# GpSimd squares and low halves in pieces of 128 columns, and a bank of the globals read by one VectorE instruction

## The chip, the core and the metric

The kernel runs on one core of one Trainium2 chip. The metric is device time in microseconds (us) of one execution, all transfers included. The engines are named as the profile names them: PE is TensorE's matmul, PEld its weight load, DVE is VectorE, ACT is ScalarE, POOL is GpSimd, SP is SyncE.

## The reference

Windowed attention with a few global tokens feeds a two-layer network whose middle is h·cos(h). Batch 8, 8 heads of 64, 512 local and 32 global positions; then 8 x 544 = 4352 tokens go through 512 -> 2048 -> 512. All inputs are float32.

```
k_all = concat([k_g, k_l]); v_all = concat([v_g, v_l])
out_g = softmax(q_g @ k_all.T / 8) @ v_all                    # 32 global rows see everything
s_ll  = where(|i - j| <= 32, q_l @ k_l.T / 8, -1e9)           # a local row sees a window
out_l = softmax(concat([q_l @ k_g.T / 8, s_ll])) @ v_all
x = concat([out_g, out_l], axis=2)      # as (tokens, 512)
h = x @ w_in                            # 512 -> 2048
return (h * cos(h)) @ w_out             # 2048 -> 512
```

## The kernel before

**Precision.** Operands are split into a float16 high and low half, and each product is made of three matmuls: high·high, high·low, low·high. So a tile that goes into a product is written twice: its high half by ScalarE, its low half by VectorE or GpSimd as value minus high half.

**Two streams that share the engines.** The attention stream works on one batch b at a time, in four pairs of heads p: scores `ps`, a masked row minimum on VectorE (the `CUSTOM_DVE_ANT_0` rows, t and mn), exponentials on ScalarE (`t<-t,mn`), the scaled probabilities in two halves (`planes`), a DMA transpose, the product with v (`acc`), which is written out as `xh` and `xl`. The globals of two pairs (g = 0 or 1) go together: scores `gps`, probabilities `gt` and `planes_g`, a DMA transpose `ptg`, and the product with v in one PSUM bank, `gacc`. The network stream takes what attention has finished in chunks c of 256 tokens (two to a batch, c = 0 to 15; c = 16 is the globals of all batches) and in 8 tiles j of 2 x 128 hidden columns. One tile (c, j), 128 x 512 values, goes through

- `m1_a`: 24 matmuls of 256 columns into a PSUM bank `ph` (three banks, so that (c, j) takes the bank of the tile three before it),
- `m1_b`, `m1_c`: `u` on ScalarE, `u` again on VectorE, the sine `w` on ScalarE (the phase of the cosine at half the angle),
- `m1_d`: the square of w on GpSimd, `gf` = (w - 0.5)·ph on VectorE, which is the last reader of the bank ph, then the high half `gh` on ScalarE and the low half `gl` = gf - gh on GpSimd,
- `m2_a`: 12 matmuls of 512 columns from gh and gl into the two banks `po`, three slots later; of each three, the third needs gl.

In the text below "square" is the GpSimd row `w<-w`, and a tile is written as its row with two numbers: gf(8, 3).

**Splitting on GpSimd.** `pool_tt(o, a, b, op, n)` issues one GpSimd instruction for each n columns. For chunks 0 and 1 n is 128 (`PSQ`, `PSG`); for c of 2 and more n is the whole width, 512.

**The bank of the globals.** `g_f` writes 40 matmuls into `gacc` as [128, pair a, half n, 32]: half 0 takes the products with the high half of the probabilities and the ones with v's low half, half 1 those with their low half. `g_g` empties it with two VectorE instructions, both of which read the bank: x = half 1 · pv, then x = half 0 · pv + x. gacc shares three banks, tag "att", with the scores: ps, gps and acc take the bank that was freed three allocations earlier.

**What sets the order.** The program is written out in slots (`at(slot, phase, f, ...)`). Their rank is a priority, and a scheduler orders the instructions of each engine by it and by its own estimate of when each can start. So an edit that changes an instruction's length can move others. Within an engine instructions then run strictly in that order.

Of the kernel before, what the change touches and what calls it, by code (L numbers as in the profile page):

```python
# [10 lines left out]
F32 = mybir.dt.float32  # L11
# [3 lines left out]
AF = mybir.ActivationFunctionType  # L15
ALU = mybir.AluOpType
AX = mybir.AxisListType
PSUM = bass.MemoryType.PSUM

P = 128  # L20
B = 8
H = 8
SL = 512
SG = 32
D = 64
NPAIR = H // 2
# [50 lines left out]
PSQ = 128  # L77
PSG = 128
# [18 lines left out]
QB = 2  # L97
QH = "A"
FB = 3
s_sc0 = -6  # L100
s_sc2 = -5
s_ex = -4
# [41 lines left out]
def body(tc, qf, v, wi, wo, mask, out):  # L144
    nc = tc.nc
    from contextlib import ExitStack

    with ExitStack() as ctx:
        cp = ctx.enter_context(tc.tile_pool(name="cp", bufs=1))
# [14 lines left out]
        for i in range(4):  # L164
            t = cp.tile([P, 2, 2, 256], F16, name=f"planes{i}")
# [13 lines left out]
        xgs = cp.tile([P, NPAIR], F32, name="xgs")  # L179
        gam = cp.tile([P, 1], F32, name="gam")  # L180
        hsc = cp.tile([P, 1], F32, name="hsc")
        osc = cp.tile([P, 1], F32, name="osc")
        xg = cp.tile([P, NPAIR, B * SG], F32, name="xg")
        pvs = cp.tile([P, B], F32, name="pvs")

        def behind(ins, what, why="scale_first"):
# [41 lines left out]
        def pool_tt(o, a, b, op, n=SPLIT):  # L228

            w = o.shape[-1]  # L230
            k = -(-w // n)
            while w % k:
                k += 1
            for i in range(k):
                c = slice(i * (w // k), (i + 1) * (w // k))
                nc.gpsimd.tensor_tensor(o[..., c], a[..., c], b[..., c], op=op)  # L236
# [302 lines left out]
        def sc_a(b, p, i):  # L539
# [3 lines left out]
            nb, np_ = (b, p + 1) if p < 3 else (b + 1, 0)  # L543
            host = i == 2 and FB <= nb < B
            pt = [
# [3 lines left out]
            if host:  # L549
                st["pmq", nb, np_] = pt[0][:, w0 + w1_ :]  # L550
            if b >= FB:
                qh, ql, kh, kl = st["qk", b, p]
# [65 lines left out]
        def sc_b(b, p, i):  # L618
# [9 lines left out]
            mn = ap_.tile([P, 2], F32, tag="mn", name=f"mn_{b}_{p}_{i}", bufs=8)  # L628
            nal = st["qs", b, p][1] if b >= FB else NAL
            for h in range(2):  # L630
# [196 lines left out]
        def g_f(b, g):  # L827
            ptg = st.pop(("ptg", b, g))
            acc = ps.tile([P, 2, 2, SG], F32, tag="att", name=f"gacc_{b}_{g}")
            for a in range(2):  # L830
                vh, vl = st["v", b, 2 * g + a]
                for tl in range(NT):
                    for ip, (vt, n) in enumerate(((vh, 2), (vl, 1))):
                        for h in range(2):
                            hh = 2 * a + h
                            mm = nc.tensor.matmul(
                                acc[64 * h : 64 * h + 64, a, :n],
                                vt[:, tl, 64 * h : 64 * h + 64],
                                ptg[:, tl : tl + NT * (n - 1) + 1 : NT, 32 * hh : 32 * hh + 32],
                                start=(a == 0 and tl == 0 and ip == 0),  # L840
                                stop=(a == 1 and tl == NT - 1 and ip == 1),
                                skip_group_check=True,
                            )
                            if b == 0 and (a, tl, ip, h) == (0, 0, 0, 0):
                                tc.add_manual_dep(mm.ins, st["pv", 0, 3].name, order, reason="globals_last")
            st["gacc", b, g] = acc

        def g_g(b, g):
            acc, pv = st.pop(("gacc", b, g)), pvs[:, b : b + 1]
            x = xg[:, 2 * g : 2 * g + 2, b * SG : (b + 1) * SG]  # L850
            nc.vector.tensor_scalar(x, acc[:, :, 1], pv, None, op0=ALU.mult)
            nc.vector.scalar_tensor_tensor(x, acc[:, :, 0], pv, x, op0=ALU.mult, op1=ALU.add)


        mp = None
# [1 line left out]
        def chunk_scales(c):  # L857
            if c < NC and c % 2:
                st["cs", c] = st["cs", c - 1]
                return  # L860
            if c < NC:
                pv = pvs[:, c // 2 : c // 2 + 1]
            else:
                pv = ap_.tile([P, 1], F32, tag="pvm", name="pvm", bufs=1)
                nc.vector.tensor_reduce(pv, pvs, axis=AX.X, op=ALU.max)
                r = ap_.tile([P, 1], F32, tag="pvr", name="pvr", bufs=1)
                inv2(r, pv)
                nc.vector.tensor_scalar(xgs, xs, r, 0.5, op0=ALU.mult, op1=ALU.mult)
                xh = ap_.tile([P, NPAIR, B * SG], F16, tag="xh", name="xh_g")
                xl = ap_.tile([P, NPAIR, B * SG], F16, tag="xl", name="xl_g")  # L870
                for p in range(NPAIR):
                    nc.scalar.activation(xh[:, p], xg[:, p], AF.Identity, scale=xgs[:, p : p + 1])
                    nc.vector.scalar_tensor_tensor(
                        xl[:, p], xg[:, p], xgs[:, p : p + 1], xh[:, p], op0=ALU.mult, op1=ALU.subtract
                    )
                st["x", c] = (xh, xl)

            a = ap_.tile([P, 1], F32, tag="ca", name=f"ca_{c}")
            m = ap_.tile([P, 1], F32, tag="cm", name=f"cm_{c}")
            o = ap_.tile([P, 1], F32, tag="co", name=f"co_{c}")  # L880
            nc.vector.tensor_scalar(a, hsc, pv, None, op0=ALU.mult)
            inv2(m, a)
            nc.vector.tensor_scalar(m, m, 2.0**90, 0.5 * MAGIC, op0=ALU.min, op1=ALU.mult)
            nc.vector.tensor_scalar(a, a, math.pi, None, op0=ALU.mult)
            nc.vector.tensor_scalar(o, osc, pv, None, op0=ALU.mult)
            st["cs", c] = (a, m, o)
# [46 lines left out]
        def m1_d(c, j):  # L933
            w = st.pop(("u", c, j))[1]
            n = w.shape[-1]
            gh = mp.tile([P, n], F16, tag="gh", name=f"gh_{c}_{j}", bufs=GB)
            gl = mp.tile([P, n], F16, tag="gl", name=f"gl_{c}_{j}", bufs=GB)
            e = SQ[NS * c + j] if c < 2 else "G"
            if e == "A":
                nc.scalar.activation(w, w, AF.Square)  # L940
            elif e == "D":
                nc.vector.tensor_tensor(w, w, w, op=ALU.mult)
            else:
                pool_tt(w, w, w, ALU.mult, PSQ if c < 2 else n)
            gf = gf_tile(c, j, n)
            nc.vector.scalar_tensor_tensor(  # L946
                gf, w, 0.5, st.pop(("ph", c, j)).rearrange("p a b -> p (a b)"),
                op0=ALU.subtract, op1=ALU.mult,
            )
            nc.scalar.copy(gh, gf)  # L950
            if c < 2 and GLE[NS * c + j] == "D":
                nc.vector.tensor_tensor(gl, gf, gh, op=ALU.subtract)
            else:
                pool_tt(gl, gf, gh, ALU.subtract, PSG if c < 2 else n)
            st["g2", c, j] = (gh, gl)

        def m2_a(c, j):
# [140 lines left out]
        for b in range(2, B):  # L1098
            t = 16 * (b - 1) + T0
# [110 lines left out]
```

## Time and profile before

| | |
|---|---|
| median of 3 runs | 956.19 us (951.73 to 956.78) |
| the profiled execution | 954.18 us, of which its span from first to last instruction is 952.4 us |
| PE busy | 886.2 us (93% of the span) |
| DVE / ACT / POOL busy | 659.6 / 682.2 / 427.5 us |
| mean granted TensorE clock | 0.981 |

A row of the time line gives the start, the length, the engine, the line of the kernel, the operation and the tiles (out<-in); `x4` at its end means that four like instructions that follow each other are put together. What stands in brackets is how long the engine sat idle before the row, and whose end released it. A matmul's length holds its latency; how fast PE works is read from the distance between starts (0.11 us for 256 columns, 0.22 us for 512).

### The profile page before, as it was taken

Reading aid. Unit: us, or ns where it says so; the run is one execution under the profiler, and the core shown is the slowest. Engines: PE = TensorE matmul, PEld = TensorE weight load, DVE = VectorE, ACT = ScalarE, POOL = GpSimd, SP = SyncE. Lnnn points to the kernel's source line nnn. Section 1 sums busy time; section 2 is a strip of 40 time slices with the busy share of each in tenths; the row PEclk is TensorE's granted clock in tenths of the full one; section 3 lists DMA queues with packets and bytes.
Section 4 is the critical chain, followed back from the end, with each engine's and each line's share of the span. In section 5 each row is a group of like instructions: output and inputs, shape, how many; then the busy total and the mean of one; then the engine's idle time right before and its main releaser. Section 6 shows DMA issues by size and latency. Waiting matters only on the chain.

```text
span 952.4 us, 20637 instructions
## 1 busy us (share of the span) xinstructions
PE 886.2 (93%) x7903; PEld 596.8 (63%) x7903; DVE 659.6 (69%) x1708; ACT 682.2 (72%) x1439; POOL 427.5 (45%) x508
## 2 busy tenths in 40 slices
PE   6757887999999999999999999999899999999995
PEld 4436564566666665666666665666566666666663
DVE  5999989757586877778786868687777765423231
ACT  6886898877787777776777778687777776434341
POOL 5867968543424243433333333424343434444441
PEclk9978999999999999999999999999999999999998
DMA  9936256655241623455352635271352433000000
GB/s 366 363 155 191 84 145 154 130 120 133 46 119 35 175 41 81 98 123 111 63 117 48 172 59 120 39 178 32 81 99 67 86 68 59 23 1 24 1 23 23
DMA packets 155179, 96.45 MB, mean 101 GB/s; under 512 B 141000, under 2 KB 141128, under 8 KB 153288
## 3 DMA queue, kind: packets, MB, share of 16 engines
q1 hardware_dynamic: 155080, 95.13, 40.4%
q8 instruction: 62, 1.02, 0.4%
q14 instruction: 37, 0.30, 0.1%
HBM read 51.59 MB, written 8.91 MB: 64 GB/s over the span
## 4 chain that ended last, share of the span: by engine, by line
PE 49%; DVE 25%; ACT 11%; DMA 6%; issue 5%; POOL 3%; SPq 0%; ACTq 0%; DVEq 0%; POOLq 0%
PE po L969 22%; PE ph L900 22%; DVE planes L679 5%; DMA vr<-v 4%; ACT t L448 4%; DVE u L923 3%; DVE t L631 2%; DVE qkr L615 2%; PE acc L731 2%; DVE gf L946 2%; DVE qm L582 2%; DMA raw_wo<-wo 2%; DVE vm L505 1%; ACT planes L678 1%; PE ps L558 1%
## 5 line engine op out<-in xcount | busy, mean ns | idle before, releaser
L969 PE MATMUL po<-wo_hl,gh 128*128 128x512 f16 x1088 | 321.7, 380 | 10.1 <-POOL wo_hl L236 9.4
L900 PE MATMUL ph<-xh,wi_h 128*128 128x256 f16 x1024 | 281.4, 275 | 6.6 <-DVE gf L946 6.6
L900 PE MATMUL ph<-xl,wi_h 128*128 128x256 f16 x1024 | 280.8, 275 | 0.5 <-DVE xl L752 0.5
L900 PE MATMUL ph<-xh,wi_l 128*128 128x256 f16 x1024 | 280.8, 275 | 0.0
L236 POOL TENSOR_TENSOR w<-w 128x512 f32<-128x512 f32 (+1 forms) x184 | 154.6, 851 | 272.5 <-ACT w L448 267.7
L236 POOL TENSOR_TENSOR gl<-gf,gh 128x512 f16<-128x512 f32 (+1 forms) x184 | 177.6, 976 | 203.2 <-ACT gh L950 202.6
L900 PEld LDWEIGHTS <-wi_h 128*128 128x128 f16 x2176 | 208.2, 98 | 55.6 <-issue 16.3
L969 PE MATMUL po<-wo_hl,gl 128*128 128x512 f16 x544 | 201.2, 380 | 0.0
L969 PEld LDWEIGHTS <-gh 128*128 128x128 f16 x1088 | 106.7, 98 | 102.9 <-issue 1.8
L448 ACT ACTIVATE w<-u,ca 128x512 f32<-128x512 f32 x136 | 98.0, 721 | 85.3 <-DVE u L923 80.9
L923 DVE SCALAR_TENSOR_TENSOR u<-u,cm,ph 128x512 f32<-128x512 f32 x136 | 100.8, 741 | 83.7 <-ACT u L922 83.7
L950 ACT CAST gh<-gf 128x512 f16<-128x512 f32 x136 | 83.1, 611 | 97.2 <-DVE gf L946 97.0
L946 DVE SCALAR_TENSOR_TENSOR gf<-w,ph 128x512 f32<-128x512 f32 x136 | 92.5, 680 | 56.7 <-POOL w L236 56.5
L448 ACT ACTIVATE t<-t,mn 128x192 f32<-128x192 f32 (+1 forms) x256 | 116.4, 456 | 6.4 <-DVE mn L631 6.1
L900 PEld LDWEIGHTS <-wi_l 128*128 128x128 f16 x1088 | 107.2, 99 | 13.7 <-issue 0.7
L679 DVE SCALAR_TENSOR_TENSOR planes<-t,sm,planes 128x192 f16<-128x192 f32 (+1 forms) x232 | 100.8, 489 | 11.3 <-ACT planes L678 10.5
L922 ACT ACTIVATE u<-ph,cm 128x512 f32<-128x512 f32 x136 | 91.7, 678 | 18.7 <-PE ph L900 18.5
L969 PEld LDWEIGHTS <-gl 128*128 128x128 f16 x544 | 53.3, 98 | 73.8 <-issue 11.6
L678 ACT ACTIVATE planes<-t,sm 128x192 f16<-128x192 f32 (+1 forms) x232 | 86.1, 455 | 11.4 <-DVE sm L651 9.2
L448 ACT ACT_TABLE_LOAD x58 | 74.4, 1283 | 12.6 <-DVE u L923 11.1
L631 DVE CUSTOM_DVE_ANT_0 t<-ps,msk,qs 128x192 f32<-128x192 f32 (+1 forms) x160 | 59.6, 427 | 1.1 <-PE ps L558 1.1
L448 ACT ACTIVATION_READ_ACCUMULATOR t<-t,mn 128x1 f32 x256 | 48.1, 188 | 0.0
(171 smaller groups left out, 1122.7 us busy)
## 6 DMA issues: line engine op xcount, KB each, us to landing
qkr<-qf SPq DMA_DIRECT2D x31, 608.0 KB, 5.7
vr<-v SPq DMA_DIRECT2D x8, 1280.0 KB, 6.7
out<-o SPq DMA_DIRECT2D x34, 256.0 KB, 2.0
raw_wi<-wi SPq DMA_DIRECT2D x6, 1024.0 KB, 12.6
wo_hl<-wo SPq DMA_DIRECT2D x8, 512.0 KB, 12.9
raw_wm<-wo SPq DMA_DIRECT2D x8, 512.0 KB, 4.4
raw_wo<-wo SPq DMA_DIRECT2D x8, 512.0 KB, 4.6
raw_wi<-wi SPq DMA_DIRECT2D x4, 512.0 KB, 12.4
```

What stands on the lines that cost most here:

```text
L236: nc.gpsimd.tensor_tensor(o[..., c], a[..., c], b[..., c], op=op)
L448: ins = nc.scalar.activation(*a, **k).ins
L582: nc.vector.tensor_reduce(m, raw.rearrange("p a b -> p (a b)"), axis=AX.X, op=ALU.max, apply_absolute_value=True)
L631: nc.vector.tensor_tensor_reduce(t[:, h], pt[h], msk[:, MOFF[i] : MOFF[i] + w], nal, 3.0e38, ALU.add, ALU.min, mn[:, h : h + 1],)
L678: a = nc.scalar.activation(hi, t[:, h], AF.Identity, scale=r)
L679: d = nc.vector.scalar_tensor_tensor(lo, t[:, h], r, hi, op0=ALU.mult, op1=ALU.subtract)
L900: nc.tensor.matmul(ph[:, a], w[:, kc, f], x[:, kc, q], start=first and ip == 0, stop=last and ip == 2, skip_group_check=True,)
L922: nc.scalar.activation(u, ph, AF.Identity, bias=m)
L923: nc.vector.scalar_tensor_tensor(u, u, m, ph, op0=ALU.subtract, op1=ALU.subtract)
L946: nc.vector.scalar_tensor_tensor(gf, w, 0.5, st.pop(("ph", c, j)).rearrange("p a b -> p (a b)"), op0=ALU.subtract, op1=ALU.mult,)
L950: nc.scalar.copy(gh, gf)
L969: nc.tensor.matmul(po[k], g[:, a * CT + k * P : a * CT + (k + 1) * P], w[:, 2 * j + a], start=(j == 0 and i == 0), stop=(j == NS - 1 and i ...
```

## The change

The squares and the low halves gl of chunks 2 to 16 are issued in pieces of 128 columns, as in chunks 0 and 1: four GpSimd instructions where there was one, 240 times. The bank gacc is laid out [128, half n, pair a, 32], so that both halves of one value stand 64 columns apart; for b of 2 and more one `tensor_reduce` adds the two halves out of the bank, and the multiplication by pv is a second VectorE instruction that works in SBUF alone (`XG` = 1; the branch with `XG` = 2 isn't taken). `xg` is laid out by batch first, and its four readers at the end are given the matching view.

```diff
@@ g_f
-                                acc[64 * h : 64 * h + 64, a, :n],
+                                acc[64 * h : 64 * h + 64, :n, a],
@@ g_g
-            x = xg[:, 2 * g : 2 * g + 2, b * SG : (b + 1) * SG]
-            nc.vector.tensor_scalar(x, acc[:, :, 1], pv, None, op0=ALU.mult)
-            nc.vector.scalar_tensor_tensor(x, acc[:, :, 0], pv, x, op0=ALU.mult, op1=ALU.add)
+            x = xg[:, b, 2 * g : 2 * g + 2].rearrange("p a b -> p (a b)")
+            hi, lo = (acc[:, k].rearrange("p a b -> p (a b)") for k in range(2))
+            if XG and b >= 2:
+                nc.vector.tensor_reduce(x, acc.rearrange("p n a b -> p (a b) n"), axis=AX.X, op=ALU.add)
+                (nc.gpsimd if XG == 2 else nc.vector).tensor_scalar(x, x, pv, None, op0=ALU.mult)
+            else:
+                nc.vector.tensor_scalar(x, lo, pv, None, op0=ALU.mult)
+                nc.vector.scalar_tensor_tensor(x, hi, pv, x, op0=ALU.mult, op1=ALU.add)
@@ m1_d
-                pool_tt(w, w, w, ALU.mult, PSQ if c < 2 else n)
+                pool_tt(w, w, w, ALU.mult, PSQ if c < 2 else PSC)
...
-                pool_tt(gl, gf, gh, ALU.subtract, PSG if c < 2 else n)
+                pool_tt(gl, gf, gh, ALU.subtract, PSG if c < 2 else PSC)
```

with `PSC = 128`. The order of instructions moves at places on DVE, ACT and POOL; PE's and SP's stay as they were but for a few rows. In the rows below a name ends with its tile (chunk and tile, or batch, pair and part) and a serial number.

VectorE where it empties the bank of batch 5's first globals, between tiles (9, 1) and (9, 2); vl is a low half of the next batch's v. Before:

```order
L946 SCALAR_TENSOR_TENSOR gf_9_1_8108<-w_9_1_8022,ph_9_1_7996 128x512
L851 TENSOR_SCALAR xg_97<-gacc_5_0_8059,pvs_98 128x2x32
L536 SCALAR_TENSOR_TENSOR vl_6_1_8654<-vr_6_7767,vs_6_7905,vh_6_1_8653 128x640
L536 SCALAR_TENSOR_TENSOR vl_6_2_9074<-vr_6_7767,vs_6_7905,vh_6_2_9073 128x640
L852 SCALAR_TENSOR_TENSOR xg_97<-gacc_5_0_8059,pvs_98,xg_97 128x2x32
L923 SCALAR_TENSOR_TENSOR u_9_2_8137<-u_9_2_8137,cm_8_7152,ph_9_2_8112 128x512
```

The same place now:

```order
L955 SCALAR_TENSOR_TENSOR gf_9_1_8453<-w_9_1_8364,ph_9_1_8338 128x512
L855 TENSOR_REDUCE xg_97<-gacc_5_0_8401 128x64
L538 SCALAR_TENSOR_TENSOR vl_6_1_9032<-vr_6_8091,vs_6_8235,vh_6_1_9031 128x640
L538 SCALAR_TENSOR_TENSOR vl_6_2_9476<-vr_6_8091,vs_6_8235,vh_6_2_9475 128x640
L856 TENSOR_SCALAR xg_97<-xg_97,pvs_98 128x64
L932 SCALAR_TENSOR_TENSOR u_9_2_8485<-u_9_2_8485,cm_8_7434,ph_9_2_8460 128x512
```

The last reader of gacc stood behind the two vl, and now stands ahead of them.

ScalarE from gh(8, 4) to the exponentials of batch 5's pair 2. Before:

```order
L950 CAST gh_8_4_7646<-gf_8_4_7649 128x512
L950 CAST gh_8_5_7719<-gf_8_5_7722 128x512
L922 ACTIVATE u_8_6_7751<-ph_8_6_7726,cm_8_7152 128x512
L448 ACTIVATE w_8_6_7752<-u_8_6_7751,ca_8_7151 128x512
L448 ACT_TABLE_LOAD
L448 ACTIVATE t_5_2_0_7708,sm_5_2_7910<-t_5_2_0_7708,mn_5_2_0_7709 128x192 x2
L448 ACTIVATE t_5_2_1_7712,sm_5_2_7910<-t_5_2_1_7712,mn_5_2_1_7713 128x224 x2
```

Now:

```order
L959 CAST gh_8_4_7958<-gf_8_4_7964 128x512
L931 ACTIVATE u_8_6_8075<-ph_8_6_8050,cm_8_7434 128x512
L450 ACTIVATE w_8_6_8076<-u_8_6_8075,ca_8_7433 128x512
L450 ACT_TABLE_LOAD
L450 ACTIVATE t_5_2_0_8026,sm_5_2_8240<-t_5_2_0_8026,mn_5_2_0_8027 128x192 x2
L450 ACTIVATE t_5_2_1_8030,sm_5_2_8240<-t_5_2_1_8030,mn_5_2_1_8031 128x224 x2
L959 CAST gh_8_5_8037<-gf_8_5_8043 128x512
```

gh(8, 5) has moved behind four exponentials, and u(8, 6) no longer stands behind it; on VectorE gf(8, 5) has moved behind u(8, 6) in the same way. Odd chunks have the same shift.

GpSimd over the same tiles. Before:

```order
L236 TENSOR_TENSOR w_8_4_7607<-w_8_4_7607 128x512
L236 TENSOR_TENSOR gl_8_3_7575<-gf_8_3_7577,gh_8_3_7574 128x512
L236 TENSOR_TENSOR w_8_5_7679<-w_8_5_7679 128x512
L820 TENSOR_TENSOR planes_g_84<-gt_5_0_7435,planes_g_84 128x544
L236 TENSOR_TENSOR gl_8_4_7647<-gf_8_4_7649,gh_8_4_7646 128x512
L236 TENSOR_TENSOR gl_8_5_7720<-gf_8_5_7722,gh_8_5_7719 128x512
L236 TENSOR_TENSOR w_8_6_7752<-w_8_6_7752 128x512
```

Now:

```order
L238 TENSOR_TENSOR w_8_4_7919<-w_8_4_7919 128x128 x4
L238 TENSOR_TENSOR gl_8_3_7881<-gf_8_3_7886,gh_8_3_7880 128x128 x4
L238 TENSOR_TENSOR w_8_5_7997<-w_8_5_7997 128x128 x3
L822 TENSOR_TENSOR planes_g_84<-gt_5_0_7735,planes_g_84 128x544
L238 TENSOR_TENSOR w_8_5_7997<-w_8_5_7997 128x128
L238 TENSOR_TENSOR gl_8_4_7959<-gf_8_4_7964,gh_8_4_7958 128x128 x4
L238 TENSOR_TENSOR w_8_6_8076<-w_8_6_8076 128x128 x4
L238 TENSOR_TENSOR gl_8_5_8038<-gf_8_5_8043,gh_8_5_8037 128x128 x4
```

Each square and gl is four rows; the last piece of the square (8, 5) stands behind planes_g, and the square (8, 6) ahead of gl(8, 5).

## Rows read from the trace of the kernel before

**Rows 1.** The head of the page: busy time of each engine, with its share of the span.

```profile
PE 886.2 (93%) x7903; PEld 596.8 (63%) x7903; DVE 659.6 (69%) x1708; ACT 682.2 (72%) x1439; POOL 427.5 (45%) x508
```

**Rows 2.** Stretches of the span: the stretch, its length, then busy us (and instructions) of each engine, PE's granted clock, the DMA share and GB/s.

```profile
320.00:440.00 120.00, 117.40 (x1103) 78.74 (x1102) 93.59 (x234) 92.14 (x202) 41.12 (x36) 0.99 0.49 108
440.00:560.00 120.00, 116.34 (x1101) 79.04 (x1101) 91.80 (x240) 91.57 (x198) 48.12 (x42) 1.00 0.38 86
560.00:680.00 120.00, 114.06 (x1110) 76.94 (x1109) 94.59 (x242) 92.09 (x193) 46.08 (x40) 1.00 0.43 93
...
800.00:943.00 143.00, 142.80 (x1024) 94.32 (x1022) 44.13 (x69) 57.62 (x88) 58.26 (x53) 1.00 0.03 12
```

**Rows 3.** What PE waited for between 200 and 800 us: us in total, times, the longest.

```profile
PE gps L781 <- DVE xg L852: 9.6, 4, 2.5
PE ph L900 <- DVE gf L946: 2.6, 3, 1.1
```

**Rows 4.** PE's time line at the longest of these waits, in chunk 9.

```profile
573.43 0.18 PE L588 MATMUL ps<-qm,ones 128*128 128x1 bf16 x1
575.96 0.31 PE L781 MATMUL gps<-qh 128*32 128x288 f16 x4 [2.36 <-DVE xg L852]
```

**Rows 5.** VectorE's time line over the same stretch.

```profile
572.86 0.28 DVE L851 TENSOR_SCALAR xg<-gacc,pvs 128x64 f32<-128x64 f32 x1
573.06 2.65 DVE L536 SCALAR_TENSOR_TENSOR vl<-vr,vs,vh 128x640 f16<-128x640 f32 x2
575.64 0.27 DVE L852 SCALAR_TENSOR_TENSOR xg<-gacc,pvs,xg 128x64 f32<-128x64 f32 x1
575.83 0.73 DVE L923 SCALAR_TENSOR_TENSOR u<-u,cm,ph 128x512 f32<-128x512 f32 x1
```

**Rows 6.** Short stretches behind two other such waits; the third number from the end is PE's granted clock.

```profile
370.00:372.00 2.00, 2.00 (x16) 1.19 (x9) 2.00 (x9) 1.78 (x2) 1.00 (x1) 0.50 0.17 60
680.00:684.00 4.00, 4.00 (x22) 2.80 (x20) 2.82 (x15) 3.97 (x13) 1.04 (x1) 0.57 0.17 66
```

**Rows 7.** PE's time line in chunk 8: the last matmul of the scores, the first into the bank that gf(8, 3) frees, and the first that needs gl(8, 3).

```profile
542.07 0.26 PE L558 MATMUL ps<-qh,qkr 64*128 64x224 f16 x1
542.93 0.27 PE L900 MATMUL ph<-xh,wi_h 128*128 128x256 f16 x1 [0.61 <-DVE gf L946]
545.98 0.38 PE L969 MATMUL po<-wo_hl,gl 128*128 128x512 f16 x1
```

**Rows 8.** The like place in chunk 9, from two time lines: gf(9, 3) on VectorE, and the first matmul into the bank that it frees.

```profile
592.80 0.68 DVE L946 SCALAR_TENSOR_TENSOR gf<-w,ph 128x512 f32<-128x512 f32 x1
594.95 0.28 PE L900 MATMUL ph<-xh,wi_h 128*128 128x256 f16 x1
```

**Rows 9.** ScalarE and VectorE in chunk 8, from their time lines: gh(8, 4), gh(8, 5); then gf(8, 4), u(8, 6), gf(8, 6) and the next long wait on VectorE.

```profile
546.46 0.62 ACT L950 CAST gh<-gf 128x512 f16<-128x512 f32 x1 [2.04 <-DVE gf L946]
548.47 0.62 ACT L950 CAST gh<-gf 128x512 f16<-128x512 f32 x1 [1.40 <-DVE gf L946]
...
545.75 0.67 DVE L946 SCALAR_TENSOR_TENSOR gf<-w,ph 128x512 f32<-128x512 f32 x1
...
549.71 0.75 DVE L923 SCALAR_TENSOR_TENSOR u<-u,cm,ph 128x512 f32<-128x512 f32 x1 [1.27 <-ACT u L922]
...
552.43 0.69 DVE L946 SCALAR_TENSOR_TENSOR gf<-w,ph 128x512 f32<-128x512 f32 x1 [0.48 <-POOL w L236]
...
556.35 0.17 DVE L650 TENSOR_SCALAR sm<-sm 128x8 f32<-128x8 f32 x1 [2.50 <-ACT t L448]
```

**Rows 10.** GpSimd's time line over the same tiles: the square (8, 4), gl(8, 3), and planes_g behind the square (8, 5).

```profile
543.18 1.04 POOL L236 TENSOR_TENSOR w<-w 128x512 f32<-128x512 f32 x1 [1.65 <-ACT w L448]
544.17 1.36 POOL L236 TENSOR_TENSOR gl<-gf,gh 128x512 f16<-128x512 f32 x1
...
546.69 1.22 POOL L820 TENSOR_TENSOR planes_g<-gt,planes_g 128x544 f16<-128x544 f32 x1
```

**Rows 11.** Lengths of VectorE instructions in ns, minimum/median/maximum: gt and planes_g of all batches; vl between 200 and 800 us; the low halves of planes in chunks 0 and 1 (88 to 200 us) and between 200 and 800 us; a reduce out of PSUM.

```profile
L818 DVE TENSOR_SCALAR gt<-gt,gsm x12: 495/994/1001, 230.7 to 791.5; 128x544 f32<-128x544 f32 x12
L819 DVE CAST planes_g<-gt x12: 433/1277/1280, 233.4 to 792.1; 128x544 f16<-128x544 f32 x12
L536 DVE SCALAR_TENSOR_TENSOR vl<-vr,vs,vh x21: 868/965/1868, 206.3 to 728.5; 128x640 f16<-128x640 f32 x21
L679 DVE SCALAR_TENSOR_TENSOR planes<-t,sm,planes x32: 404/548/889, 123.8 to 182.2; 128x192 f16<-128x192 f32 x16, 128x224 f16<-128x224 f32 x16
L679 DVE SCALAR_TENSOR_TENSOR planes<-t,sm,planes x192: 398/436/1311, 201.5 to 790.8; 128x192 f16<-128x192 f32 x96, 128x224 f16<-128x224 f32 x96
L515 DVE TENSOR_REDUCE vs<-pm_v x8: 274/282/292, 18.8 to 662.8; 128x1 f32<-128x128 f32 x8
```

**Rows 12.** GpSimd's time line in chunks 0 and 1, where a square or a gl is four pieces already; the length is from the start of the first to the end of the last.

```profile
102.72 1.47 POOL L236 TENSOR_TENSOR w<-w 128x128 f32<-128x128 f32 x4
...
110.98 1.92 POOL L236 TENSOR_TENSOR w<-w 128x128 f32<-128x128 f32 x4
112.86 1.59 POOL L236 TENSOR_TENSOR gl<-gf,gh 128x128 f16<-128x128 f32 x4
```

**Rows 13.** The end: the last gl on GpSimd, and PE at the product that needs it, from two time lines.

```profile
937.39 1.15 POOL L236 TENSOR_TENSOR gl<-gf,gh 128x512 f16<-128x512 f32 x1 [1.45 <-ACT gh L950]
940.04 1.03 PE L969 MATMUL po<-wo_hl,gh 128*128 128x512 f16 x4
```

More of the change, by code (lines that the diff above doesn't have):

```diff
@@ L99 @@
 FB = 3
+PSC = 128
+XG = 1
 s_sc0 = -6
@@ L182, in body @@
         osc = cp.tile([P, 1], F32, name="osc")
-        xg = cp.tile([P, NPAIR, B * SG], F32, name="xg")
+        xg = cp.tile([P, B, NPAIR, SG], F32, name="xg")
         pvs = cp.tile([P, B], F32, name="pvs")
@@ L871, in chunk_scales @@
                 for p in range(NPAIR):
-                    nc.scalar.activation(xh[:, p], xg[:, p], AF.Identity, scale=xgs[:, p : p + 1])
+                    xp = xg[:, :, p]
+                    xhp, xlp = (t[:, p].rearrange("p (a b) -> p a b", a=B) for t in (xh, xl))
+                    nc.scalar.activation(xhp, xp, AF.Identity, scale=xgs[:, p : p + 1])
                     nc.vector.scalar_tensor_tensor(
-                        xl[:, p], xg[:, p], xgs[:, p : p + 1], xh[:, p], op0=ALU.mult, op1=ALU.subtract
+                        xlp, xp, xgs[:, p : p + 1], xhp, op0=ALU.mult, op1=ALU.subtract
                     )
```

## The prediction

> **What bounds the kernel now.** I read the stages first, then what PE waits for, then the time lines around those waits. By busy time PE leads with 93%, the others stand at 45 to 72% [rows 1]. The stages show where the rest is: from 800 us on PE is busy all the time and VectorE, ScalarE and GpSimd are under half; between 320 and 680 us it sits idle for 2.60 + 3.66 + 5.94 = 12.2 us [rows 2]. So PE's work sets the end, and each idle microsecond of PE before 680 us is paid at the end, for the tail has none to give back. Two waits make up that idle time [rows 3]. (a) Four times, once in each batch, the globals' second scores wait for VectorE's xg: after the row at 573.43 PE starts gps at 575.96, so it stands 2.53 us, four times about 10.1 us; the page counts 9.6, since it takes off the latency of the matmul before [rows 4]. (b) Three times ph waits for gf(c, 3) of an even chunk, up to 1.1 us, 2.6 us in all [rows 3, 7].
>
> Behind two of the four waits (a) PE's granted clock is 0.50 for some microseconds and then 1.00 again [rows 6]: 1.2 GHz in place of 2.4. The stretch from 680 to 684 us stands at 0.57, so PE lost some 0.43·4 = 1.7 us of work there; the first is at least 1.0 us (2 us at 0.50) and by its like 1.7. Rows 3 don't count these 3.4 us, as PE counts as busy in them. What PE could win in all is 12.2 + 3.4 = 15.6 us.
>
> The second reading is whether the engines that feed PE would let it. VectorE and ScalarE hand each tile to and fro, and at the places (b) it is they that are late. In chunk 9, behind the wait (a), gf(9, 3) ends at 593.48 and PE takes its bank at 594.95: 1.47 us to spare [rows 8]. In chunk 8 there is nothing to spare: PE is done with the scores at 542.2 and takes the bank at 542.93, as gf(8, 3) ends [rows 7]. So PE alone can use 1.47 us of the 2.53 before it stands at gf(9, 3) instead. Only if VectorE and ScalarE come sooner as well is the wait gone for good: by 2.53 + 1.1 = 3.6 us for each batch, 1.8 for each chunk.
>
> **The change, part by part.** *The globals' bank.* Before, the first xg ends at 573.14, two vl take 2.65 us, and the second xg, the bank's last reader, ends at 575.91; PE starts 0.05 us later [rows 4, 5]. Now the reduce is the only reader and stands where the first xg stood. It reads 128 values of a partition from PSUM, as the reduce of L515 does in 0.28 us [rows 11]; the first xg took 0.28 too [rows 5]. So the bank is free at about 573.15, before PE asks for it at 573.5. The wait (a) goes: -10.1 us, and -3.4 us for the clock if it fell because PE stood. The scaling of xg in SBUF, 0.2 to 0.3 us, replaces the second xg one for one. The end reads xg with strides in four ScalarE and four VectorE instructions, while PE is full [rows 2]: nothing. PE writes gacc's halves 64 columns apart; the same columns, nothing.
>
> The VectorE page of the Trainium skill (VectorE: DVE Perf Modes, Rules for kernel authors) calls a reduce the slowest of VectorE's operations and advises against it on a hot path. By the row, at 128 values it costs no more than what it replaces; by the rule, at 2 or 4 times 0.28 us, the bank would be free at 574.0 at the latest, and 0.5 us of the four waits would stay.
>
> *The pieces, their price on GpSimd.* Undisturbed, a square takes 1.04 us whole [rows 10] and 1.47 in pieces, a gl 1.15 whole [rows 13] and 1.59 in pieces [rows 12]: +0.43 each, 240·0.43 = 103 us more work for an engine that is busy 427 of 952 us [rows 1]. Where VectorE cuts in, a square of four pieces took 1.92 us [rows 12]. GpSimd has room on average; what counts is the one burst in each chunk, the squares (c, 4) and (c, 5), gl(c, 3) to gl(c, 5) and planes_g.
>
> *What the pieces take off VectorE.* VectorE rows that work in SBUF alone stretch when GpSimd runs. gt takes 0.50 us alone and 0.99 in the median, planes_g 0.43 and 1.28, two vl took 2.65 where twice the shortest is 1.74 [rows 5, 11]. In time the stretch ends when GpSimd's instruction ends: planes_g's 1.28 us lies over a gl of 1.36 [rows 10]. A piece lasts a quarter, 1.47/4 = 0.37 us. So gt and planes_g, 2.27 us in the median, become 0.93 plus at most two pieces, 0.93 to 1.67; I take 1.4, -0.9 us for each chunk. The two vl of odd chunks go from 2.65 to 1.74 plus at most two pieces, so to 2.1: -0.55 us. The lo halves of planes lose as much as they win: in chunks 0 and 1, with pieces, their median is 0.55 against 0.44 later, but their longest is 0.89 against 1.31 [rows 11].
>
> *The new order.* u(8, 6) on ScalarE stood behind gh(8, 5), which waited 1.40 us for gf(8, 5); so VectorE got to its u(8, 6) at 549.71 after 1.27 us idle [rows 9]. Now u(8, 6) follows gh(8, 4). The square (8, 4) starts at 543.18 [rows 10]; four pieces with two VectorE rows between take 1.92 [rows 12], so it ends at 545.1; gf(8, 4), 0.67 us, ends at 545.8, gh(8, 4), 0.62 us, at 546.4; u on ScalarE is about 0.7 us, so VectorE's u(8, 6) can start at 547.2, 2.5 us sooner. Not all of it is kept: gf(8, 5) now waits for the last piece of its square, which stands behind gl(8, 3) and planes_g: 545.1 + 1.59 + 1.47 + 1.22 = 549.4, and the scores' rows behind gf(8, 5) come at 550.1, about 0.3 sooner than before. But the exponentials that don't need these start 2.5 us sooner, and what is lost between is gh(8, 5)'s 0.62 us, now among them: I take -1.8 us for the chunk's ScalarE stream. gf(8, 6), later by some 1.5 us, lies under VectorE's wait of 2.50 us before sm [rows 9]; without that cover it would cost 1.5.
>
> *Sum for the feeding engines.* About -1.8 us for each chunk, and -0.55 more in odd ones: as much as PE needs (1.8). So most of the 15.6 us is reached, and PE is the bound almost throughout.
>
> *What it costs PE.* gl(c, 3) is later. gl(8, 3) ended at 545.53, 2.6 us after PE took the bank that gf(8, 3) had freed [rows 7, 10]; now its square ahead ends at 545.1 and gl takes 1.59 to 1.92: 546.7 to 547.0, some 3.9 us after it. PE needs it at 545.98, 3.05 us after it [rows 7]. Where PE takes the bank just as gf frees it, it stands 0.85 us; four even chunks: +3.4 us. Where PE comes later, nothing. At the end the last gl is later by 0.86, and there is 1.50 us between it and its product [rows 13]: nothing.
>
> **Sum.** Against the profiled 954.2 us: -10.1 (a) - 2.6 (b) - 3.4 (clock) + 3.4 (gl) = -12.7, so 941.5. The clock need not fall in each execution, so I count half of its 3.4: 943.2. The median of the runs shown, 956.19, lies 2.0 above the profiled one and the fastest 2.5 below; I leave the sum at **943 us** and put that scatter into the range.
>
> **Rivals.** *R1, the feeding engines don't come sooner* (piece for piece VectorE loses what it wins, as at the planes): PE then stands at gf(c, 3) instead of at xg. What stays is the 1.47 us to spare in the last batch: 952.7, no change that can be told. For it: chunk 8 already stands at gf [rows 7]. Against: the longest stretches are cut, and u(8, 6) is no longer behind gh(8, 5).
> *R2, the squares' delay sets VectorE's pace, slower.* gf(8, 6) starts as its square ends, with VectorE idle before it [rows 9]; I take three such tiles in a chunk. A square in pieces ends 0.43 us later, 0.88 where VectorE cuts in (1.92 against 1.04) [rows 10, 12], and all that VectorE has in order behind gf waits with it. Three times 0.88 is 2.6 us for each chunk against the 1.8 won: 0.8 us times some 10 chunks, less R1's 1.5: about 961 us. It decides as soon as what the waits for squares add to a chunk is more than what the shorter stretches and the new order take off. The skill's page SBUF — State Buffer (Who interferes with whom) has a rule on this side: the two engines share one pair of ports, and whichever instruction starts first holds it to its end while the other stands. The trace agrees, since planes_g's 1.28 us ends with GpSimd's instruction [rows 10, 11]. By that rule a square cut in four can be held up at each of its cuts by a VectorE row, where the whole one was held up once.
> *R3, the bank isn't freed sooner in effect* (gps turns out to wait for another reader of the three banks): (a) stays, (b) goes: 954.2 - 2.6 = 951.6. Against: PE starts 0.05 us after xg's end in the row.
>
> **Chances.** 0.5% is 4.8 us, about what a measurement of this kernel can tell from no change. The forecast (under 951.4) 0.68; R1 and R3 together 0.18, within 0.5%; R2 0.14, slower. The forecast's own range is 938 (all 15.6 us won, with the runs' scatter 937) to 949. To hold 8 in 10 the range must take in R1 and R3 and their scatter: 937 to 956; R2 is left out.
>
> **What would show it.** No wait of gps for xg; PE idle between 320 and 680 us under 4 us; no stretch at clock 0.5 there; the reduce at 0.28 us; gt and planes_g together near 1.4 us; squares of four pieces at 1.5 to 1.9 us; VectorE's wait for u(c, 6) gone. Wrong would be: the wait of ph for gf(c, 3) grown to 2 us and more (R1), many waits of VectorE's gf for squares before 680 us (R2), or PE standing at the product for gl(c, 3) in every chunk.

## The result and the profile after

The changed kernel takes 938.42 us (median of 5 runs, 938.05 to 939.10) against 954.23 us (5 runs, 951.73 to 956.78): 0.983 of the time before, 95% interval 0.981 to 0.985. The profiled execution took 938.54 us with a span of 936.7. Busy time of each engine, the line that answers to [rows 1]:

```profile
PE 883.8 (94%) x7903; PEld 596.1 (64%) x7903; DVE 648.1 (69%) x1708; ACT 683.0 (73%) x1439; POOL 540.6 (58%) x1228
```

GpSimd has 113 us more to do (427.5 before), and PE, which sets the end, doesn't wait for it. The stages of [rows 2], in the same columns:

```profile
320.00:440.00 120.00, 119.88 (x1132) 80.74 (x1130) 96.53 (x248) 94.16 (x200) 62.45 (x150) 1.00 0.47 106
440.00:560.00 120.00, 120.00 (x1170) 81.64 (x1169) 92.28 (x245) 98.04 (x210) 67.72 (x162) 1.00 0.43 94
560.00:680.00 120.00, 119.90 (x1147) 81.33 (x1146) 94.01 (x254) 98.46 (x212) 63.99 (x153) 1.00 0.42 99
```

PE's idle time between 320 and 680 us is down from 12.2 us to 0.22. From 200 to 800 us PE waits for nobody in the view of waits, where [rows 3] had 9.6 and 2.6 us, and the stretches at half clock of [rows 6] are gone: from 154 to 931 us the granted clock is 1.00. That is all there was to win (12.2 + 3.4 = 15.6), and the span fell by 15.7 us (952.4 to 936.7).

So far it looks as if the globals' bank had done it. VectorE and PE at the place of [rows 4, 5], in chunk 9 of the changed kernel (start, length, engine, line):

```profile
561.54 0.28 DVE L855 TENSOR_REDUCE xg<-gacc 128x64 f32<-128x128 f32 x1
561.75 1.97 DVE L538 SCALAR_TENSOR_TENSOR vl<-vr,vs,vh 128x640 f16<-128x640 f32 x2
563.64 0.41 DVE L856 TENSOR_SCALAR xg<-xg,pvs 128x64 f32<-128x64 f32 x1
...
564.65 0.18 PE L590 MATMUL ps<-qm,ones 128*128 128x1 bf16 x1
564.76 0.31 PE L783 MATMUL gps<-qh 128*32 128x288 f16 x4
```

The reduce ends at 561.82, 2.9 us before gps. But the scaling, which stands where the second reader stood, ends at 564.05, also ahead of gps, by 0.7 us. VectorE has come so much sooner that a second reader would have been in time. Whose doing that is the profile of this one kernel can't say; the runs below do.

ScalarE in chunk 8, at the place of [rows 9]:

```profile
537.00 0.62 ACT L959 CAST gh<-gf 128x512 f16<-128x512 f32 x1 [1.52 <-DVE gf L955]
537.52 0.68 ACT L931 ACTIVATE u<-ph,cm 128x512 f32<-128x512 f32 x1
539.09 0.72 ACT L450 ACTIVATE w<-u,ca 128x512 f32<-128x512 f32 x1 [0.88 <-DVE u L932]
539.83 1.28 ACT L450 ACT_TABLE_LOAD   x1
...
542.94 0.60 ACT L959 CAST gh<-gf 128x512 f16<-128x512 f32 x1
```

u(8, 6) follows gh(8, 4) at once, and the table load for the exponentials starts at 539.83, 2.86 us after the end of gf(8, 4) (536.97); before it was 4.88 us (551.30 after 546.42, where gf(8, 4) of [rows 9] ends). gh(8, 5), the last row, no longer holds up u(8, 6). The table load of the kernel before:

```profile
551.30 1.28 ACT L448 ACT_TABLE_LOAD   x1
```

### The profile page after: what moved, and what is told of

Read it like the earlier page. It is cut to its first block, busy times and chain, and to the rows that moved or that the text cites. A ratio compares the mean times of both kernels' runs of the same rounds, so it can differ in the third digit from the quotient of the medians.

```text
span 936.7 us, 21428 instructions
## 1 busy us (share of the span) xinstructions
PE 883.8 (94%) x7903; PEld 596.1 (64%) x7903; DVE 648.1 (69%) x1708; ACT 683.0 (73%) x1439; POOL 540.6 (58%) x1228
## 3 DMA queue, kind: packets, MB, share of 16 engines
q8 instruction: 62, 1.02, 0.4%
## 4 chain that ended last, share of the span: by engine, by line
PE 73%; DVE 10%; ACT 6%; DMA 4%; POOL 4%; issue 3%; SPq 0%; ACTq 0%; POOLq 0%
PE ph L909 32%; PE po L978 32%; PE acc L733 3%; PE ps L560 3%; DMA vr<-v 2%; DVE planes L681 2%; ACT t L450 1%; DMA raw_wo<-wo 1%; DVE u L932 1%; PE gacc L838 1%; ACT planes L680 1%; PE gps L783 1%; PE ps L573 1%; DVE gf L955 1%; POOL w L238 1%
## 5 line engine op out<-in xcount | busy, mean ns | idle before, releaser
L238 POOL TENSOR_TENSOR gl<-gf,gh 128x128 f16<-128x128 f32 x544 | 233.2, 463 | 180.6 <-ACT gh L959 180.6
L238 POOL TENSOR_TENSOR w<-w 128x128 f32<-128x128 f32 x544 | 214.4, 426 | 168.6 <-ACT w L450 166.7
L681 DVE SCALAR_TENSOR_TENSOR planes<-t,sm,planes 128x192 f16<-128x192 f32 (+1 forms) x232 | 95.4, 464 | 6.7 <-ACT planes L680 6.5
L733 PE MATMUL acc<-pt,vh 128*64 128x128 f16 (+3 forms) x768 | 45.5, 239 | 3.0 <-ACT pt L698 3.0
## 6 DMA issues: line engine op xcount, KB each, us to landing
raw_wi<-wi SPq DMA_DIRECT2D x4, 512.0 KB, 12.2
```

Source lines behind the costliest of these rows:

```text
L681: d = nc.vector.scalar_tensor_tensor(lo, t[:, h], r, hi, op0=ALU.mult, op1=ALU.subtract)
L733: mm = nc.tensor.matmul(acc[64 * h : 64 * h + 64, q_out : q_out + n0 * len(segs)], vt[:, tl, 64 * h : 64 * h + 64], rhs, start=(k == 0 and ...
```

## The experiments

Eleven kernels, each timed in five rounds beside the kernel before on the same chip (its medians were 954.51, 953.08 and 954.50 us):

| kernel | us, median | ratio, 95% interval |
|---|---|---|
| bank alone | 951.88 | 0.9975 (0.9954 to 0.9995) |
| pieces and their order, bank read twice | 938.56 | 0.9836 (0.9806 to 0.9865) |
| bank and pieces, gh(c, 5) first again | 957.16 | 1.0039 (1.0019 to 1.0058) |
| order alone, both halves | 937.97 | 0.9832 (0.9804 to 0.9859) |
| order, gh's half alone | 944.59 | 0.9910 (0.9887 to 0.9932) |
| order, the planes' half alone | 943.83 | 0.9874 (0.9849 to 0.9898) |
| order in even chunks alone | 942.99 | 0.9899 (0.9876 to 0.9923) |
| order in odd chunks alone | 945.50 | 0.9920 (0.9894 to 0.9947) |
| order and bank | 938.34 | 0.9842 (0.9816 to 0.9869) |
| pieces, gh late, planes as before | 940.53 | 0.9844 (0.9820 to 0.9869) |
| pieces in nearly the old order | 958.93 | 1.0046 (1.0027 to 1.0065) |

### The two parts of the diff, one at a time

Bank alone:

```diff
-PSC = 128
+PSC = 512
```

> The changed kernel with whole squares and whole gl of 512 columns; the globals' bank is still emptied by the one reduce. The order on ScalarE, GpSimd and SyncE is that of the kernel before. Theory A (the prediction's): the bank's second reader is what PE stands for, but PE can use only the 1.47 us that VectorE and ScalarE have to spare; the wait of gps for xg is gone and the waits of ph for gf(c, 3) of even chunks grow; 952.7 us, at most 1% faster. Theory B: the bank alone is the cause, VectorE and ScalarE come sooner as soon as PE does; 954.2 - 10.1 - 3.4 = 940.7 us, with no wait of PE left but the 2.6 us for gf.

Measured 951.88 us: theory A. The waits of PE from 200 to 800 us (who for whom, us in total, times, longest):

```profile
PE ph L909 <- DVE gf L955: 9.1, 7, 1.7
PE ph L909 <- DVE xl L754: 1.0, 4, 0.3
```

The wait for xg is gone and 10 us of waits for VectorE's other rows have taken its place (and 0.6 us for one gl). The bank alone is worth a quarter of a per cent. In the two profiled executions it is 4.9 us (954.18 to 949.31): 1.5 us less of PE's waits (12.2 to 10.7) and the two stretches at half clock, 3.4 us, which don't occur here.

Pieces alone, with the bank read twice:

```diff
-XG = 1
+XG = 0
```

> The changed kernel with pieces of 128 columns, but the globals' bank read twice by VectorE as before (the order on PE, ScalarE, GpSimd and SyncE is that of the changed kernel). Theory A (the prediction's sum): what the bank gave comes back, four waits of gps for the second reading of 2.5 us, and the clock behind two of them; 938.5 + 10.1 to 13.5 = 949 to 952 us. Theory C: in the trace of the changed kernel the scaling that stands in the second reader's place ends at 564.05 us and gps starts at 564.76, so a second reader there would be in time by 0.7 us; the pieces and the new order alone remove the wait, 938 to 941 us.

Measured 938.56 us: theory C, as fast as the changed kernel, with no wait of PE. VectorE in chunk 9:

```profile
562.85 0.28 DVE L858 TENSOR_SCALAR xg<-gacc,pvs 128x64 f32<-128x64 f32 x1
563.04 1.97 DVE L538 SCALAR_TENSOR_TENSOR vl<-vr,vs,vh 128x640 f16<-128x640 f32 x2
564.94 0.27 DVE L859 SCALAR_TENSOR_TENSOR xg<-gacc,pvs,xg 128x64 f32<-128x64 f32 x1
```

The second reader ends 0.5 to 0.9 us before gps in the four batches. With the order of the changed kernel the bank is worth nothing.

### The order against the pieces

The scheduler had answered the pieces with another order of instructions. First the changed kernel with the old place of gh(c, 5):

```diff
-            nc.scalar.activation(u, ph, AF.Identity, bias=m)
+            ua = nc.scalar.activation(u, ph, AF.Identity, bias=m)
+            if 3 <= c <= 11 and j == 6:
+                tc.add_manual_dep(ua.ins, st["gh_ins"], order, reason="gh_first")
...
-            nc.scalar.copy(gh, gf)
+            st["gh_ins"] = nc.scalar.copy(gh, gf).ins.name
```

> The changed kernel (pieces, one reduce), but on ScalarE u(c, 6) stands behind gh(c, 5) again in chunks 3 to 11, as before. Theory A (the prediction's steps): the order was worth 1.8 us of the feeding engines' time in a chunk and the shorter stretches about 1.2; PE needs 1.8, so 0.6 us are short in each chunk and PE stands for gf(c, 3) of even chunks by about 1.2 us, four times and again some 1 us for the clock: 943 to 946 us. Theory D: the shorter stretches on VectorE alone suffice and the order is worth nothing: 938.5 us, no wait of PE. If the order is worth more than 1.8, the wait of gps or ph grows to 3 us a batch: 950 us.

Measured 957.16 us, slower than the kernel before, though both parts of the diff are in it, and above what any of the theories had: PE waits 8.0 us for gf and 2.0 for qkr. Either the order is worth far more than 1.8 us a chunk, or the pieces do harm without it. (The scheduler answers this edit too: u(c, 7) moves ahead of qh.)

Then the order alone: whole instructions and the bank read twice, the copy gh(c, 5) issued behind the sine of (c, 6).

```diff
-            nc.scalar.copy(gh, gf)
+            if 3 <= c <= 11 and j == 5:
+                st["gh_later"] = (gf, gh, gl)
...
+            if j == 6 and "gh_later" in st:      # in m1_c, behind the sine
+                gf, gh, gl = st.pop("gh_later")
+                cp_ = nc.scalar.copy(gh, gf)
+                tc.add_manual_dep(cp_.ins, ins.name, order, reason="sin_first")
+                pool_tt(gl, gf, gh, ALU.subtract, PSC)
```

> The order alone: whole squares and whole gl, the globals' bank read twice as before, but in chunks 3 to 11 gh(c, 5) stands behind u(c, 6) and its sine on ScalarE, as in the changed kernel (its exponentials stay behind it). Theory A: worth up to 1.8 us in a chunk for the feeding engines, 3.6 in a batch, which is what the waits of gps and of ph add up to; most of both waits goes: 941 to 946 us. Theory D: the order is worth nothing without the pieces, since VectorE is still held up beside GpSimd: 953 to 955 us, the waits of gps for xg still 2.5 us. A third way, slower: gl(c, 5) is later by 2 us and PE stands for it: above 956 us.

Measured 937.97 us, better than the 941 to 946 expected: the whole gain, without a single piece and without the reduce. PE waits 0.2 us in all. ScalarE in this kernel at two places of chunk 8, and below it the kernel before at the second place:

```profile
537.22 0.68 ACT L931 ACTIVATE u<-ph,cm 128x512 f32<-128x512 f32 x1
539.44 0.72 ACT L450 ACTIVATE w<-u,ca 128x512 f32<-128x512 f32 x1 [1.53 <-DVE u L932]
540.07 0.60 ACT L943 CAST gh<-gf 128x512 f16<-128x512 f32 x1
540.69 1.28 ACT L450 ACT_TABLE_LOAD   x1
...
547.90 0.67 ACT L753 ACTIVATE xh<-acc,xs 128x512 f16<-128x512 f32 x1
548.47 1.17 ACT L680 ACTIVATE planes<-t,sm 128x192 f16<-128x192 f32 x3
549.68 1.28 ACT L450 ACT_TABLE_LOAD   x1
550.97 0.72 ACT L450 ACTIVATE w<-u,ca 128x512 f32<-128x512 f32 x1
```

```profile
557.94 0.67 ACT L922 ACTIVATE u<-ph,cm 128x512 f32<-128x512 f32 x1
558.51 0.67 ACT L751 ACTIVATE xh<-acc,xs 128x512 f16<-128x512 f32 x1
560.29 1.28 ACT L448 ACT_TABLE_LOAD   x1 [1.11 <-DVE u L923]
561.58 0.72 ACT L448 ACTIVATE w<-u,ca 128x512 f32<-128x512 f32 x1
```

Two things differ. At the first place u(8, 6) doesn't wait behind gh(8, 5), and the table load comes 4.02 us after the end of gf(8, 4) in place of 4.88. At the second place ScalarE stood 1.11 us for VectorE's u(8, 7) before it could load the sine's table; now three hi halves of planes lie in that time. The scheduler had moved them as a consequence of the first move; the changed kernel has them there as well.

### The two halves of the order

gh's place alone is the kernel above with the planes held behind the sine of (c, 7); against the kernel before it moves on ScalarE those nine copies and nothing else. On GpSimd the square (c, 6) comes ahead of gl(c, 5) as well, nine times, since gl needs gh; VectorE's and PE's orders are as before.

```diff
+            st["sin", c, j] = ins.name
...
+                    sn = st.get(("sin", 2 * b - (2 if p == 2 else 3), 7))
+                    if b >= 3 and p in (0, 2) and sn:
+                        tc.add_manual_dep(a.ins, sn, order, reason="sin_first")
```

> The kernel before (whole instructions, the bank read twice) with nine instructions of ScalarE moved and no others: gh(c, 5) of chunks 3 to 11 stands behind u(c, 6) and its sine. In the kernel with the order alone the scheduler had also put three of planes' seven hi halves ahead of the table load for the sine of (c, 7), where ScalarE had stood 1.1 us for VectorE's u; here they are held behind that sine as before. From the two traces: from the end of gf(8, 4) to the end of gh(8, 6) it is 10.40 us before and 9.55 with the order alone, so gh's place is worth 0.85 us a chunk; the three planes, 1.37 us of ScalarE's time, go into the 1.1 us that it stood, so they are worth up to 1.1 to 1.4. PE needs 1.8 a chunk. Theory E: both moves are needed, gh's place alone gives 1.7 of 3.6 us a batch: 945 to 949 us, gps still waits for xg by about 1 us. Theory F: gh's place is all of it, 937 to 940 us, no wait of PE.

Measured 944.59 us. The planes' half alone (the sine and the square of (c, 7) issued behind the planes, gh as before):

```diff
-                at(s + 1, mc, m1_c, c, j)
-                at(s + 1, md, m1_d, c, j)
+                hold = 4 <= c <= 11 and j == 7
+                at(s + 1, PF + 0.5 if hold else mc, m1_c, c, j, pr=(s + 1, mc))
+                at(s + 1, PF + 0.6 if hold else md, m1_d, c, j, pr=(s + 1, md))
```

> The kernel before with the other half of the order and no more: in chunks 4 to 11 three of planes' seven hi halves (both of t 0, the first of t 1) stand ahead of the table load and the sine of (c, 7), with VectorE's three lo halves; gh(c, 5) stays ahead of u(c, 6). Whole instructions, the bank read twice. Theory E: ScalarE had stood 1.1 us there for VectorE's u, so the three, 1.37 us, cost little in that place: 1.1 to 1.4 us a chunk of the 1.8 that PE needs, 941 to 945 us; gh's place alone gave 8.5 us of 15. If the planes are of use only behind gh's move, 952 to 955 us.

Measured 943.83 us. PE's waits from 200 to 800 us, of gh's half and then of the planes' half:

```profile
PE gps L786 <- DVE xg L862: 5.9, 4, 1.6
```

```profile
PE gps L784 <- DVE xg L860: 4.8, 4, 1.4
```

Theory E holds in both, with gh's half 0.4 us below its range. The length of a stretch of the chunk shows the same. Here are u(9, 0) before (its gf(8, 4) is in [rows 9]), then gf(8, 4) and u(9, 0) with gh's half, then with the planes' half:

```profile
565.80 0.67 ACT L922 ACTIVATE u<-ph,cm 128x512 f32<-128x512 f32 x1
...
539.63 0.68 DVE L964 SCALAR_TENSOR_TENSOR gf<-w,ph 128x512 f32<-128x512 f32 x1
558.83 0.67 ACT L934 ACTIVATE u<-ph,cm 128x512 f32<-128x512 f32 x1
...
538.38 0.67 DVE L958 SCALAR_TENSOR_TENSOR gf<-w,ph 128x512 f32<-128x512 f32 x1
557.38 0.67 ACT L932 ACTIVATE u<-ph,cm 128x512 f32<-128x512 f32 x1
```

In the even chunk 8 the end of gf(8, 4) and the start of u(9, 0) lie 19.37 us apart before, 18.52 with gh's half (-0.85), 18.33 with the planes' half (-1.04) and 17.46 with both (-1.91). In the odd chunk 9, from the end of gf(9, 4) to the end of gf(10, 3), it is 48.57 us before, 47.52 (-1.05), 47.13 (-1.44) and 46.30 with both (-2.27). The halves nearly add, and together they pass the 1.8 us that PE needs in a chunk.

Next both halves in one kind of chunk:

```diff
-            if 3 <= c <= 11 and j == 5:
+            if c in (4, 6, 8, 10) and j == 5:          # the other kernel: c in (3, 5, 7, 9, 11)
```

> The order alone, in the even chunks 4, 6, 8 and 10 only (gh(c, 5) behind u(c, 6) and its sine, and with it three planes ahead of the table load); odd chunks stand as before. By theory E a chunk in the new order gives 2.0 to 2.3 us (0.85 and 1.1 to 1.4) and PE needs 3.6 in a batch of two chunks: 1.3 to 1.6 us a batch are short, in waits of gps or of ph, so 943 to 947 us. If the loss arose in the even chunks alone: 938 us; if in the odd ones alone: 953 us.

> The order alone, in the odd chunks 3, 5, 7, 9 and 11 only; even chunks stand as before. As with the even ones, by theory E: 943 to 947 us, with waits of 1.3 to 1.6 us a batch. If the loss arose in the odd chunks alone: 938 us; if in the even ones alone: 953 us.

Measured 942.99 and 945.50 us, both between 943 and 947 but for a hundredth: half the order leaves about two fifths of PE's waits (5.2 and 4.6 us of 12.2). The loss arose in even and odd chunks alike, though its largest wait, (a), came once a batch.

Order and bank together (the order's edit with XG = 1 and whole instructions):

> The order and the bank's one reduce, whole instructions. If PE is the bound once the order has changed, neither the pieces nor the bank have anything left to give: 937 to 939 us, as the changed kernel and as the order alone (937.97). If the bank still takes away what the order leaves (one wait of 0.2 us for xg in its trace) it is 0.2 us, not to be measured. If the pieces were of use apart from the order, this kernel is slower than the changed one, 941 us and more.

Measured 938.34 us, no wait of PE. With PE full, neither bank nor pieces have anything left to give. No kernel here beats the changed one by more than the measurement tells; the order alone equals it with 114 us less work on GpSimd (426.3).

### What the pieces do by themselves

The pieces while VectorE and ScalarE still set the pace: the kernel with pieces and the bank read twice, with the planes held behind the sine by the edit shown above.

> The pieces of 128 columns, the bank read twice, gh(c, 5) where the changed kernel has it, but the three planes held behind the sine of (c, 7) as before. Against gh's place alone with whole instructions (944.59 us) this shows what the pieces themselves do while VectorE and ScalarE still set the pace. Theory A (the prediction's): the shorter stretches on VectorE give 0.9 us in an even and 1.45 in an odd chunk, which with gh's 0.85 is what PE needs: 938 to 940 us. Theory N, the pieces change nothing: 944 to 946 us. Theory S (the prediction's rival R2): later squares take more than the stretches give, 947 to 952 us.

Measured 940.53 us, near theory A: 4 us better than gh's half with whole instructions (0.7% by the ratios, since the two were timed beside different runs of the kernel before). That this is the pieces' own doing isn't shown: with them gh(c, 5) stands behind four exponentials too, and VectorE has u(c, 6) ahead of gf(c, 5). The runs don't separate these.

The pieces in nearly the old order (the edit that keeps gh first, for j 6 and 7, and the held planes):

> The pieces of 128 columns in nearly the old order: gh(c, 5) and gh(c, 6) ahead of u(c, 6) and u(c, 7) in chunks 3 to 11, the three planes behind the sine of (c, 7), the bank read twice; some other neighbours on ScalarE and VectorE stand as the scheduler puts them for pieces. Theory A: the shorter stretches alone give 0.9 and 1.45 us a chunk, 2.35 of the 3.6 us of a batch: 944 to 947 us. Theory N: 953 to 955 us. Theory S: slower than before, as the pieces with the bank in the old order of gh were 5.3 us above the bank alone: 957 to 961 us, with waits of PE for gf or xg grown.

Measured 958.93 us, in theory S's range. GpSimd and ScalarE of this kernel in chunk 8:

```profile
546.00 1.58 POOL L238 TENSOR_TENSOR gl<-gf,gh 128x128 f16<-128x128 f32 x4
547.55 1.10 POOL L238 TENSOR_TENSOR w<-w 128x128 f32<-128x128 f32 x3
548.62 1.21 POOL L825 TENSOR_TENSOR planes_g<-gt,planes_g 128x544 f16<-128x544 f32 x1
549.80 0.39 POOL L238 TENSOR_TENSOR w<-w 128x128 f32<-128x128 f32 x1
...
546.79 0.62 ACT L965 CAST gh<-gf 128x512 f16<-128x512 f32 x1 [1.52 <-DVE gf L961]
550.94 0.62 ACT L965 CAST gh<-gf 128x512 f16<-128x512 f32 x1 [3.53 <-DVE gf L961]
551.47 0.68 ACT L934 ACTIVATE u<-ph,cm 128x512 f32<-128x512 f32 x1
553.76 1.28 ACT L450 ACT_TABLE_LOAD   x1
```

The last piece of the square (8, 5) comes behind planes_g, so gf(8, 5) ends 4.15 us after gf(8, 4) where it was 2.02 before. gh(8, 5) waits 3.53 us, u(8, 6) with it, and the table load comes 7.0 us after gf(8, 4) against 4.88. In the changed kernel gf(8, 5) is just as late (4.16 us), but nothing on ScalarE waits for it, as gh(8, 5) stands behind four exponentials there.

So the pieces in this order do harm. The stretches measured above are 19.40 us in chunk 8 (19.37 before) and 49.87 in chunk 9 (48.57 before): in the even chunk gain and loss cancel, in the odd one the loss is larger. How much of it is the pieces' own length, and how much the place of planes_g (1.21 us) between them and of other neighbours on VectorE, no run separates. In the order of the changed kernel none of this reaches PE.

## Why the prediction was right, and where not

The time was predicted at 943 and came out at 938.4, inside the range; the sign and the bound were right, and 11.2 us were forecast of the 15.8 that were measured. That it came so near is in part luck: the largest term stands under the wrong part, about half of what ScalarE gained came by a move that the prediction didn't see, and two terms (gl, and half of the clock) were too cautious. Step by step:

**PE is the bound, and 15.6 us can be won.** Right: idle time 12.2 to 0.22 us, the clock's 3.4 us as well. I had counted half of these; with the waits gone there was no stretch at half clock between 154 and 931 us.

**PE can use a freed bank only if VectorE and ScalarE come sooner.** Right, and the most useful step: rival R1's 952.7 us, worked out from the 1.47 us to spare, is near what the bank alone measured (951.88). Its 1.5 us of PE's time came as worked out; the clock, which R1 left out, gave the rest.

**"The wait (a) goes: -10.1 us", by the reduce.** The step that failed. The forecast wrote the largest term to the bank. With the new order the second reader is in time by 0.5 to 0.9 us, and the kernel without the reduce is as fast. The bank was where the loss showed. It came from ScalarE, which stood for VectorE in each chunk: in chunk 8 for 1.40 us before gh(8, 5) [rows 9] and for 1.11 before the sine's table load. The order that goes round both waits gives PE the 1.8 us a chunk that it needs. The prediction held both numbers and took them as two conditions, "and", without asking whether the second made the first needless: 3.6 us sooner in a batch is more than the 2.53 that PE stood there.

**The new order, -1.8 us a chunk.** In size near what both halves give (-1.91 and -2.27), but half of it for another reason. gh's place is worth 0.85 to 1.05 in a kernel of whole instructions. The other half, the planes ahead of the sine's table load (1.04 to 1.44), I had not seen: I followed ScalarE's order over some eight rows and stopped ahead of this place. In the changed kernel the even chunks gain 2.34 us; the odd chunk 9 is about as long as before (48.42 us), and u(9, 6) waits 1.0 us for PE's ph there. Between 200 and 800 us ScalarE's waits for ph rose from 4.4 to 16.9 us, the sign that the feeding engines have room.

**The pieces shorten VectorE's stretches, -0.9 and -0.55 us.** The durations came as said or better, by the rows that answer to [rows 11] (minimum, median and longest in ns, count 12):

```profile
L820 DVE TENSOR_SCALAR gt<-gt,gsm x12: 487/498/504, 229.8 to 774.7; 128x544 f32<-128x544 f32 x12
L821 DVE CAST planes_g<-gt x12: 436/522/526, 232.6 to 775.2; 128x544 f16<-128x544 f32 x12
```

gt and planes_g take 1.02 us together (1.4 said, 2.27 before), two vl 1.97 (2.1 said, 2.65 before). Yet in nearly the old order, with the neighbours that the scheduler gave them there, the pieces cost 0.46%: what the stretches gave was gone again behind the late gf(c, 5). That is the mechanism of R2, and the prediction had its rows (squares of four pieces at 1.92; the burst's is 2.01 here). R2 failed as a forecast: u(c, 6) no longer stands behind gh(c, 5), so the late gf(c, 5) holds up less.

The sign that the prediction named for R2 did come. VectorE's waits for squares from 200 to 680 us, before and in the changed kernel:

```profile
DVE gf L946 <- POOL w L236: 6.8, 13, 1.2
DVE gf L955 <- POOL w L238: 21.4, 36, 2.0
```

They are three times as long (3.9 us in the order alone), and PE still waits for nobody. VectorE's waits count only if they reach PE, so the sign could not decide for R2 or against it.

One reading of the rows was loose. The prediction has planes_g end with GpSimd's gl(8, 3), at 545.53 [rows 10]:

```profile
544.55 1.28 DVE L819 CAST planes_g<-gt 128x544 f16<-128x544 f32 x1
```

It ends at 545.83, 0.30 us behind gl: the stretch ends with gl, and some of the row's own work follows.

Squares of four pieces took 1.47 us undisturbed and 2.01 in the burst, where VectorE's gt and planes_g run beside them. The rule on the shared ports in the Trainium skill, SBUF — State Buffer (Who interferes with whom), fits these lengths. The Trainium skill's page VectorE: DVE Perf Modes (Rules for kernel authors) calls the reduce the slowest operation; no run here shows that at 128 values, where it took 284 ns in the median, as much as each of the two readers before (0.28 and 0.27 us).

**gl(c, 3), +3.4 us.** Mis-sized: nothing. GpSimd and PE in chunk 8 of the changed kernel:

```profile
536.21 1.59 POOL L238 TENSOR_TENSOR gl<-gf,gh 128x128 f16<-128x128 f32 x4
...
537.20 0.38 PE L978 MATMUL po<-wo_hl,gl 128*128 128x512 f16 x1
```

gl's last piece ends at 537.80, 0.6 us after PE's first product with gl has begun, and PE doesn't stand: this product reads 128 columns of gl, one piece, which is long done. I had let PE wait for the whole of gl. With this term at nothing and the clock in full the sum is -10.1 - 2.6 - 3.4 = -16.1, so 938.1; the total is PE's idle time and doesn't depend on who removes it.

## What to carry to other kernels

Where a change lets a scheduler choose, the new order is a part of the change of its own: follow it on each engine through a whole period, and run it alone. A wait that shows once a period can be the sum of small delays in all of it; removing its nearest cause then moves most of it to the next row, as the bank alone did. When two steps both remove one wait, ask what each would do without the other before writing the gain to either.

## What the runs showed of the hardware that was not expected

- A piece of a GpSimd instruction frees its own columns: PE's product with 128 columns of gl began 0.6 us before the last of four pieces had ended.
- Cutting a square of 512 columns into four costs GpSimd 0.43 us undisturbed (1.04 to 1.47) and up to 0.97 in the burst (2.01), and the scheduler may place another instruction of 1.2 us between the pieces.
- A short row on VectorE stretches too. In the bank alone, where GpSimd's instructions are whole, the scaling of xg in SBUF, 64 columns, took 242 to 254 ns each time that GpSimd was idle and up to 1148 where it ran; with pieces it takes 413 in the median. The reduce out of PSUM stayed at 282 to 292 ns in both kernels, with GpSimd running or not. The scaling in the bank alone (minimum, median and longest in ns):

```profile
L856 DVE TENSOR_SCALAR xg<-xg,pvs x12: 242/374/1148, 264.2 to 816.2; 128x64 f32<-128x64 f32 x12
```

- The clock fell to half for 3.4 us in the middle of the kernel before (twice), of the kernel with gh first again (twice) and of the pieces in nearly the old order (three times), whose longest waits of PE are 2.5, 1.7 and 1.7 us; in the bank alone, with waits as long as 1.7 us, and in gh's half alone, up to 1.6, it never did. So the longest wait doesn't decide it alone; what does stays open here.
